# Clustered attention: staging of head pairs doubled, the first pair's load and argmax split, and a new order

## The chip, the cores and the metric

The kernel runs on one core of a Trainium2 chip, as one launch. The metric is device microseconds. Before the change three runs took 733.81, 740.06 and 740.70 us, median 740.06.

## The reference

Attention of 2 x 8 heads over 768 positions of 64 numbers, in which a query sees only the keys that were assigned to its cluster, followed by two feed-forward layers:

```python
q_assign = np.argmax(np.einsum('bhsd,hcd->bhsc', q_n, c_n), axis=-1)   # 16 clusters
k_assign = np.argmax(np.einsum('bhsd,hcd->bhsc', k_n, c_n), axis=-1)
mask = q_assign[:, :, :, None] == k_assign[:, :, None, :]
scores = np.where(mask, scale * np.matmul(q, k.transpose(0, 1, 3, 2)), -1000000000.0)
scores = scores - np.max(scores, axis=-1, keepdims=True)
attn = np.exp(scores); attn = attn / (np.sum(attn, axis=-1, keepdims=True) + 1e-09)
out = np.matmul(attn, v)
x = max(x @ w1, x @ w2, x @ w3) @ w_out      # 1536 tokens, 512 -> 768 -> 512
x = relu(x @ w_in) ** 2 @ w_out2             # 512 -> 2048 -> 512
```

## The kernel before

The 16 heads are worked on as eight pairs of 128 partitions (two heads of 64). Numbers are split into a rounded part and a remainder, and each product is made of several matmuls over the parts. All changes lie in the attention stage; the feed-forward layers behind it stay as they are.

For each pair p:

1. SP loads queries and keys (tq, tk, L284) and values (tv, L291). The first pair comes in two halves.
2. rq, rk round queries (times 0.125) and keys into rl (L343, L350), lq, lk make the remainders (L359, L365). rl has one buffer, and so have tq and tk.
3. Eight DMAs on SP (L375 to L378) copy rl into the two stacks, ste for the even head and stodd for the odd one, in which a head's rounded part and remainder lie on the two halves of the partitions.
4. TensorE multiplies rl with the centroids (sim, L404, two halves of six matmuls), ScalarE scales the result (simc, L409), TensorE transposes it (argt, L420), VectorE takes the argmax in five steps (arg0 to arg4, L427 to L448), TensorE transposes the one-hot result (mkt, L457; for the first pair also mkk, L462). ScalarE turns it into mask rows m (m4, L472), which SP copies into the stacks (md, L479 to L482). For the first even head they are written to the stack directly (L470, L471).
5. Each of the 12 score tiles of a pair (S, L497 and L499) takes two matmuls without and two with the mask rows. VectorE takes the row maximum (L506), ScalarE the exponential with its sum (L513). For a group of three tiles VectorE adds the guard 1e-9 to the sums (L517) and takes the reciprocal (L518). GpSimd normalizes (nrm, L528), TensorE transposes (T, L533, three at a time into one bank), ScalarE rounds (hi, L539), VectorE makes the remainder (lo, L544), and TensorE multiplies with the values (av, L553 and L554). ScalarE copies the result out (avt), GpSimd adds its halves (xr, L575) and writes it to xT (xh, xl, L581 and L587), the input of the next layer.

xT holds 4 head pairs x 2 parts x 1536 tokens. A pair of the first batch writes the first 768 tokens, one of the second batch the others.

What sets the order: the steps are put into a table of operations with their dependencies and buffers (room), and a planner in the program gives each engine's instructions their order when the program is built, by the keys in OFF and the durations in COST and COST2. On the chip each engine then works in that order, and SP and ScalarE issue their DMAs in it. warm(n) issues n small matmuls that nobody reads, with counts from WARM.

Of the kernel before, what the change touches and what calls it, by code (L numbers as in the profile page):

```python
# [45 lines left out]
}  # L46
COST = {
    "ldqk": ("sp", 0.95, 2.18), "ldv": ("sp", 0.48, 1.09), "stack": ("sp", 2.6, 3.28), "md": ("sp", 2.6, 0.55),
    "wld": ("sp", 0.95, 2.91), "clr": ("pool", 1.35, LAT), "scl": ("pool", 0.25, LAT),
    "sim": ("pe", 0.97, 0.2), "argt": ("pe", 0.35, 0.2), "mkt": ("pe", 0.35, 0.2), "S": ("pe", 0.65, 0.2),  # L50
    "T": ("pe", 0.33, 0.2), "av": ("pe", 0.33, 0.2), "m": ("pe", 0.65, 0.2),
    "simc": ("act", 0.46, LAT), "m4": ("act", 0.88, LAT), "ex": ("act", 0.88, LAT), "hi": ("act", 0.37, LAT),
    "avt": ("act", 0.75, LAT), "arg0": ("dve", 0.47, LAT), "arg1": ("dve", 0.47, LAT), "arg2": ("dve", 0.27, LAT),
    "arg3": ("dve", 0.47, LAT), "arg4": ("dve", 0.47, LAT), "mx": ("dve", 0.87, LAT), "rec": ("dve", 0.3, LAT),
    "xr": ("pool", 0.96, LAT), "xh": ("pool", 0.8, LAT), "xl": ("pool", 0.96, LAT),
# [29 lines left out]
def clustered_attention_moe(ctx, tc, qT, kT, vv, cen, w123, wo1, win, wo2, out):  # L85
# [154 lines left out]
    with ExitStack() as actx:  # L240
# [86 lines left out]
        for a, b in zip_longest(norm, parts):  # L327
            a()
            if b is not None:
                b()  # L330
# [631 lines left out]
```

## Time and profile before

| | |
|---|---|
| timed runs | 733.81, 740.06, 740.70 us |
| the profiled execution | 735.72 us, of it span 733.8 us |
| TensorE busy | 709.2 us (97%), mean granted clock 0.988 |
| VectorE busy | 577.5 us (79%) |
| GpSimd busy | 450.0 us (61%) |
| ScalarE busy | 328.9 us (45%) |

The page's busy time is an average over stages. Attention takes roughly the first 270 us. In it four engines work in turn on every group of tiles; behind it TensorE works alone for the most part. A matmul's span reaches from its start to its modelled end and overlaps the next one's, so TensorE can be called busy where it is not at its peak. Clock 1.00 stands for 2.4 GHz and 0.50 for 1.2 GHz.

### The profile page before, as it was taken

The numbers are of one execution on the slowest core, as the hardware profiler recorded it, in microseconds if no ns is written. First come the engines' busy times: TensorE is split into PE (matmuls) and PEld (weight loads), VectorE is DVE, ScalarE is ACT, GpSimd is POOL, SyncE is SP. The second block draws the span as 40 slices with busy tenths as digits, with TensorE's granted clock in tenths as the row PEclk, the third lists the DMA queues.
The fourth block names the chain that finished last, engine by engine and source line by source line (L and its number), as shares of the span: only waits on it lengthen the run. The fifth ranks groups of instructions, "written<-read, shape, count | busy, mean of one in ns | idle before, by whom it ended". The sixth has DMA issues, their size and how long they took to land.

```text
span 733.8 us, 10401 instructions
## 1 busy us (share of the span) xinstructions
PE 709.2 (97%) x3640; PEld 599.0 (82%) x3640; DVE 577.5 (79%) x946; ACT 328.9 (45%) x630; POOL 450.0 (61%) x385
## 2 busy tenths in 40 slices
PE   6879999899999999999999999999999999999998
PEld 5678988788898878888888888878888888888886
DVE  6788999799999999888988586795766777665434
ACT  4678898788989852222122112232222222323210
POOL 4546985988678767446654243376777666766540
PEclk9799999999999999999999999999999999999999
DMA  7756537355454002213221122202111111210004
GB/s 169 177 149 149 123 94 190 64 145 121 112 135 155 2 1 87 86 58 115 86 80 53 56 72 86 87 32 84 58 57 59 58 57 58 89 55 1 0 1 172
DMA packets 20244, 63.00 MB, mean 86 GB/s; under 512 B 3200, under 2 KB 3968, under 8 KB 19168
## 3 DMA queue, kind: packets, MB, share of 16 engines
q1 hardware_dynamic: 20192, 62.34, 29.8%
q8 instruction: 29, 0.48, 0.3%
q14 instruction: 23, 0.19, 0.1%
HBM read 38.83 MB, written 3.15 MB: 57 GB/s over the span
## 4 chain that ended last, share of the span: by engine, by line
PE 76%; DVE 11%; ACT 3%; SPq 3%; DMA 3%; POOL 2%; issue 2%; ACTq 0%; DVEq 0%; POOLq 0%
PE psd L236 27%; PE pss L876 18%; PE pss L236 14%; PE pss L533 4%; DVE nm L506 3%; PE psd L497 3%; PE pss L553 3%; PE pss L554 2%; PE psd L499 2%; DVE at L544 2%; PE pss L404 2%; DMA stodd<-rl 2%; POOL e L528 1%; ACT e L513 1%; SPq L377 1%
## 5 line engine op out<-in xcount | busy, mean ns | idle before, releaser
L211 POOL TENSOR_TENSOR wt<-wt,ww 128x512 f32<-128x512 f32 (+1 forms) x56 | 78.6, 1413 | 118.1 <-DVE wt L210 118.1
L876 PE MATMUL pss<-w,g 128*128 128x512 f32 (+1 forms) x582 | 134.8, 390 | 1.8 <-DVE acc L882 1.8
L236 PE MATMUL psd<-xT,whl 128*128 128x512 f32 x432 | 131.2, 390 | 0.1
L876 PEld LDWEIGHTS pss<-w,g 128*128 128x128 f32 x582 | 109.6, 190 | 24.9 <-DVE acc L882 2.3
L884 DVE TENSOR_TENSOR acc<-pss,acc 128x512 f32<-128x512 f32 (+1 forms) x85 | 58.2, 684 | 79.7 <-PE pss L876 79.6
L236 PE MATMUL psd<-yT,whl 128*128 128x512 f32 x384 | 118.3, 389 | 0.0
L544 DVE TENSOR_TENSOR at<-pss,at 128x384 fp32r<-128x384 f32 x192 | 100.1, 545 | 9.1 <-ACT at L539 7.9
L533 PE MATMUL pss<-ident,e 128*128 128x128 f32 x576 | 94.5, 275 | 6.5 <-DVE at L544 3.3
L539 ACT CAST at<-pss 128x384 fp32r<-128x384 f32 x192 | 88.3, 479 | 23.5 <-PE pss L533 19.7
L528 POOL TENSOR_SCALAR e<-e,nm 128x768 f32<-128x768 f32 x93 | 86.5, 947 | 15.5 <-DVE nm L518 12.3
L506 DVE TENSOR_REDUCE nm<-psd 128x1 f32<-128x768 f32 x96 | 90.5, 946 | 5.8 <-PE psd L499 5.3
L236 PEld LDWEIGHTS psd<-xT,whl 128*128 128x128 f32 x432 | 80.6, 188 | 16.8 <-POOL xT L587 0.5
L513 ACT ACTIVATE e<-psd,nm 128x768 f32<-128x768 f32 x96 | 87.3, 910 | 12.9 <-DVE nm L506 11.9
L533 PEld LDWEIGHTS pss<-ident,e 128*128 128x128 f32 x576 | 73.2, 141 | 16.9 <-DVE at L544 5.3
L236 PEld LDWEIGHTS psd<-yT,whl 128*128 128x128 f32 x384 | 72.1, 188 | 15.0
L899 ACT ACTIVATE rt<-psd 128x1024 f32<-128x1024 f32 x16 | 16.5, 1029 | 143.5 <-PE psd L236 141.1
L224 POOL TENSOR_TENSOR whl<-wt,whl 128x512 fp32r<-128x512 f32 (+1 forms) x40 | 58.5, 1463 | 36.1 <-ACT whl L223 36.1
L236 PE MATMUL pss<-xT,whl 128*128 128x512 f32 x216 | 80.5, 389 | 0.0
L904 POOL TENSOR_TENSOR g<-rt,g 128x768 fp32r<-128x768 f32 x32 | 67.4, 2128 | 16.4 <-ACT g L902 16.4
L553 PE MATMUL pss<-at,vs 128*128 128x384 f32 x192 | 75.2, 392 | 0.1
L236 PE MATMUL pss<-yT,whl 128*128 128x512 f32 x192 | 74.7, 389 | 0.0
L554 PE MATMUL pss<-at,vs 128*128 128x384 f32 x192 | 65.4, 340 | 1.4 <-DVE at L544 1.3
(121 smaller groups left out, 1198.2 us busy)
## 6 DMA issues: line engine op xcount, KB each, us to landing
wr<-w SPq DMA_DIRECT2D x16, 512.0 KB, 3.4
wr<-wo SPq DMA_DIRECT2D x16, 512.0 KB, 3.4
wr<-win SPq DMA_DIRECT2D x16, 512.0 KB, 3.7
ste<-rl SPq DMA_DIRECT2D x8, 576.0 KB, 4.9
ste<-rl SPq DMA_DIRECT2D x24, 192.0 KB, 5.3
stodd<-rl SPq DMA_DIRECT2D x8, 576.0 KB, 6.1
stodd<-rl SPq DMA_DIRECT2D x24, 192.0 KB, 5.9
tv<-vv SPq DMA_DIRECT2D x8, 384.0 KB, 4.3
```

Of the source, the lines that this page charges most:

```text
L211: lambda: pool.tensor_tensor(t, t, f(w), op=ALU.add),
L236: pe.matmul(pt[n], w[:, wi, c], x[:, k, xi, ch(n)], start=first and wi + xi == 0, stop=last and wi == 1)
L506: dve.tensor_reduce(nms[g][:, 0, i : i + 1], pss[s][:, :, :HS], axis=AX.XY, op=ALU.max, negate=True)
L513: act.activation(two(e), pss.pop(s)[:, :, :HS], AF.Exp, bias=nm[:, 0, i : i + 1], accum_out=nm[:, 1, i : i + 1])
L528: (pool if w == "P" else dve).tensor_scalar(e, e, r, 1.0, op0=ALU.mult, op1=ALU.mult)
L533: pe.transpose(pt[:, i * P : (i + 1) * P], et[3 * g + i][:, kt * P : (kt + 1) * P], ident)
L539: act.copy(a[:, 0, :], pts[g, kt][:, :HS])
L544: eng.tensor_tensor(a[:, 1, :], pts.pop((g, kt))[:, :HS], f(a[:, 0, :]), op=ALU.subtract)
L553: pe.matmul(avs[g][:, :HS], l, a[:, 0, :], start=kt == 0, stop=False)
L554: pe.matmul(avs[g][:, :HS], l, a[:, 1, :], start=False, stop=kt == NQ - 1)
L876: pe.matmul(pt[:, n], gs[fi][:, a, c], wspl[u_out(fi)][:, wi, n], start=fi == fs[0] and a + wi == 0, stop=fi == fs[-1] and a == 1)
L904: todo.append(lambda h=h, fi=fi: (pool).tensor_tensor(gt[:, 1, h], rt[:, h], f(gt[:, 0, h]), op=ALU.subtract))
```

## The change

- tq, tk, the mask rows (sm) get two buffers, at six for four. Odd pairs are staged (rl) in the part of xT for the second batch's tokens of head pairs 2 and 3, which only pairs 6 and 7 write.
- The first pair's two key loads go to ScalarE's DMA queue.
- The first even stack's own half is copied by ScalarE and GpSimd (own), its other half by two DMAs instead of four in all; later pairs' eight DMAs alternate between the even and the odd stack, the remainders first.
- The first pair's argmax, its transposes and its mask rows are made in two halves. The centroid norms (cn) become an operation of the planner. The first pair's lk is split between VectorE and GpSimd.
- The guard's addition goes from VectorE to ScalarE (ra).
- Warm-up matmuls: 12, 10, 36, 17 become 12, 10, 0, 20, 12, 8.
- The planner's durations and all its keys have new values.

```diff
-WARM = 12, 10, 36, 17, 0
+WARM = 12, 10, 0, 20, 12, 8, 0
-    "lk@0": "D", ...
+    "lk@0": "DP", ...
 OFF = {
-    "ldqk": -0.85, "ldv": 11.9, "ldqk+@0": 0.5, ...
+    "ldqk": 20.52, "ldv": -58.87, "ldqk+@0": 109.58, ...
 ...
+    guard = cp.tile([P, 1], F32, name="guard")
+    pool.memset(guard, 1e-9)
 ...
-                ins[p] = [ap.tile([P, S], F32, tag=t, bufs=1, name=f"{t}{p}") for t in ("tq", "tk")]
+                ins[p] = [ap.tile([P, S], F32, tag=t, bufs=2, name=f"{t}{p}") for t in ("tq", "tk")]
-            for t, src in zip(ins[p], (qT, kT)):
-                sp.dma_start(t[:, c], src[b, hp][:, c])
+            for t, src, q in zip(ins[p], (qT, kT), (sp, act if p == 0 else sp)):
+                q.dma_start(t[:, c], src[b, hp][:, c])
 ...
+                if p % 2:
+                    prep[p] = xT[:, 2:4].rearrange("p h i n -> p (h i) n")[:, :, S:]
+                else:
+                    prep[p] = ap1.tile([P, 4, S], F32R, tag="rl", name=f"rl{p}")
 ...
+        def p_own(p, i):
+            rl, t = prep[p], stack_of(p, 0)
+            if i == 0:
+                act.copy(t[0:64, 0:2, :], f(rl[0:64, 0, :]).unsqueeze(1).to_broadcast([64, 2, S]))
+            else:
+                pool.tensor_scalar(t[0:64, 2:4, :], f(rl[0:64, 1:3, :]), 1.0, 1.0, op0=ALU.mult, op1=ALU.mult)
+        def p_stack(p, *os):
+            rl = prep[p]
+            ts = {o: stack_of(p, o) for o in os}
+            for i in range(2 if p == 0 and os == (0,) else 4):
+                for o, t in ts.items():
+                    lo, hi = slice(64 * o, 64 * o + 64), slice(64 - 64 * o, 128 - 64 * o)
+                    to, fr = [((hi, 0), (lo, 3)), ((hi, 2), (lo, 1)), ((lo, slice(1, 4)), (lo, slice(0, 3))), ((lo, 0), (lo, 0))][i]
+                    sp.dma_start(f(t[to]), f(rl[fr]))
 ...
+        def tiles_of(hf):
+            t = range(NQ) if hf is None else range(NQ // 2 * hf, NQ // 2 * (hf + 1))
+            return t, slice(4 * t[0], 4 * t[-1] + 4)
 ...
+        def p_mq(p, hf):
+            act.activation(st[0][64:80, 1, half(hf)], pmk[p][0:16, half(hf)], AF.Identity, bias=m4b[0:16], scale=m4s[0:16])
+        def p_mk(p, hf):
+            dve.tensor_copy(st[0][64:80, 3, half(hf)], pmk["k"][0:16, half(hf)])
 ...
+        def a_guard(g):
+            nm = nms[g]
+            act.activation(nm[:, 2, :], nm[:, 1, :], AF.Identity, bias=guard)
         def a_rec(g):
             nm = nms[g]
-            dve.tensor_scalar_add(nm[:, 2, :], nm[:, 1, :], 1e-9)
             dve.reciprocal(nm[:, 3, :], nm[:, 2, :])
 ...
-            a = ap.tile([P, 2, HS], F32R, tag="at", bufs=4, name=f"at{g}_{kt}")
+            a = ap.tile([P, 2, HS], F32R, tag="at", bufs=6, name=f"at{g}_{kt}")
 ...
-        room = {"S": 2, ..., "at": 4, ..., "rl": 1, "clr": 2, "tqk": 1, ..., "sm": 1, ...}
+        room = {"S": 2, ..., "at": 6, ..., "rl": 2, "clr": 2, "tqk": 2, ..., "sm": 2, ...}
```

The start of ScalarE's instructions, before (cs are the centroid norms, table the loading of a function table, rl the first pair's staging, simt the scaled similarities):

```order
L114 ACT_TABLE_LOAD
L114 ACTIVATE table<-tiny 128x1
L314 ACTIVATE cs<-cs,tiny 128x1
L345 ACTIVATE rl_169<-tq_163 128x384 x2
L354 ACT_TABLE_LOAD
L354 ACTIVATE table<-tiny 128x1
L409 ACTIVATE simt_200<-pss_72,scl 64x384
L409 ACTIVATE simt_200<-pss_73,scl 64x384
```

and now:

```order
L118 ACT_TABLE_LOAD
L118 ACTIVATE table<-tiny 128x1
L319 ACTIVATE cs<-cs,tiny 128x1
L289 DMA tk_159<-kT 128x384 x2
L351 ACTIVATE rl_170<-tq_158 128x384 x2
L360 ACT_TABLE_LOAD
L360 ACTIVATE table<-tiny 128x1
L383 CAST ste_180<-rl_170 64x1536
```

The key loads stand behind the square root for cs, and the copy of the stack's own half ahead of the similarities.

GpSimd from the rounding of a new pair's queries on, before (rl_333 is pair 1, rl_521 pair 2, e_339 the third tile of the first group, e_343 to e_384 the second group, vs_382 the values of pair 1):

```order
L343 TENSOR_SCALAR rl_333<-tq_297 128x768
L350 TENSOR_SCALAR rl_333<-tk_298 128x768
L365 TENSOR_TENSOR rl_333<-tk_298,rl_333 128x384 x2
L528 TENSOR_SCALAR e_339<-e_339,nm_315 128x768
L383 TENSOR_SCALAR vs_382<-tv_335 128x6x2x64
L391 TENSOR_TENSOR vs_382<-tv_335,vs_382 128x3x128
L528 TENSOR_SCALAR e_343<-e_343,nm_337 128x768
L528 TENSOR_SCALAR e_369<-e_369,nm_337 128x768
L528 TENSOR_SCALAR e_384<-e_384,nm_337 128x768
L391 TENSOR_TENSOR vs_382<-tv_335,vs_382 128x3x128
L343 TENSOR_SCALAR rl_521<-tq_442 128x768
```

and now (rl_371 is pair 2, staging in xT pair 3, e_375 the third tile of the first group, e_379 to e_450 the second group):

```order
L349 TENSOR_SCALAR rl_371<-tq_249 128x768
L356 TENSOR_SCALAR rl_371<-tk_250 128x768
L371 TENSOR_TENSOR rl_371<-tk_250,rl_371 128x384
L399 TENSOR_SCALAR vs_398<-tv_334 128x6x2x64
L566 TENSOR_SCALAR e_375<-e_375,nm_323 128x768
L407 TENSOR_TENSOR vs_398<-tv_334,vs_398 128x3x128 x2
L371 TENSOR_TENSOR rl_371<-tk_250,rl_371 128x384
L566 TENSOR_SCALAR e_379<-e_379,nm_373 128x768
L566 TENSOR_SCALAR e_424<-e_424,nm_373 128x768
L566 TENSOR_SCALAR e_450<-e_450,nm_373 128x768
L349 TENSOR_SCALAR xT<-tq_388 128x768
L356 TENSOR_SCALAR xT<-tk_389 128x768
```

The same place among the normalizations now holds the staging of the pair after: pair 2 where pair 1 stood, pair 3 where pair 2 stood.

SP now, behind the eight copies of pair 1's stacks (tq_388 is pair 3, tq_458 pair 4, tv_441 the values of pair 2, m_485 the mask rows of pair 1); before, only pair 2's two loads stood between those copies and the mask rows:

```order
L289 DMA tq_388<-qT 128x768
L289 DMA tk_389<-kT 128x768
L296 DMA tv_441<-vv 128x768
L289 DMA tq_458<-qT 128x768
L289 DMA tk_459<-kT 128x768
L514 DMA ste_344<-m_485 16x768
L515 DMA ste_344<-m_485 16x768
L516 DMA stodd_133<-m_485 16x768
L517 DMA stodd_133<-m_485 16x768
```

The mask rows of pair 1 have moved behind three more loads.

## Rows read from the trace of the kernel before

**Rows 1.** Stages: us, busy of each engine (instructions), clock, DMA share, GB/s.

```profile
0.00:16.05 16.05, 10.44 (x107) 8.09 (x107) 10.40 (x43) 7.33 (x11) 7.88 (x25) 1.00 0.67 165
16.05:30.54 14.49, 11.74 (x40) 8.95 (x41) 8.19 (x10) 7.46 (x15) 5.75 (x7) 0.65 0.66 164
30.54:46.91 16.37, 11.74 (x83) 10.32 (x81) 12.73 (x25) 11.16 (x25) 7.39 (x8) 1.00 0.90 220
46.91:69.09 22.18, 21.87 (x142) 19.67 (x142) 20.69 (x39) 19.42 (x44) 13.90 (x17) 1.00 0.62 144
69.09:222.03 152.94, 148.72 (x962) 132.55 (x962) 141.13 (x256) 134.40 (x296) 124.50 (x132) 0.99 0.50 118
128.60:162.40 33.80, 31.07 (x194) 27.57 (x193) 27.73 (x52) 26.89 (x60) 29.57 (x32) 0.95 0.48 113
192.69:222.03 29.34, 29.14 (x194) 26.32 (x194) 27.45 (x52) 26.69 (x60) 24.87 (x28) 1.00 0.46 101
222.03:272.69 50.66, 48.52 (x306) 42.38 (x306) 48.35 (x88) 42.84 (x96) 37.70 (x38) 1.00 0.16 57
272.69:733.80 461.11, 456.12 (x2009) 377.00 (x2008) 335.97 (x490) 106.30 (x148) 252.89 (x163) 1.00 0.19 66
```

**Rows 2.** Chain of waits, 49.52 to 54: start us, us on the chain, what.

```profile
49.52 0.33 PE pss L533 x3
...
51.92 0.35 PE psd L497 x2
52.27 0.35 PE psd L499 x2
52.62 1.05 PE pss L404 x6
53.67 0.18 PE pss L553
```

**Rows 3.** Timeline of TensorE: start us, us, instruction, idle before and its releaser.

```profile
9.66 2.18 PE L128 MATMUL pss<-identb 128*128 128x128 bf16 x36
...
16.05 0.59 PE L497 MATMUL psd<-ste 128*128 128x384 f32 x2 [1.37 <-issue]
```

**Rows 4.** Timeline of GpSimd, the rounding of loaded keys (L350) and queries (L343).

```profile
6.61 0.51 POOL L350 TENSOR_SCALAR rl<-tk 128x384 fp32r<-128x384 f32 x1 [1.83 <-DMA tk<-kT]
...
24.18 0.83 POOL L343 TENSOR_SCALAR rl<-tq 128x768 fp32r<-128x768 f32 x1 [10.72 <-DMA stodd<-m]
...
44.10 0.83 POOL L343 TENSOR_SCALAR rl<-tq 128x768 fp32r<-128x768 f32 x1 [8.57 <-DMA ste<-m]
...
129.49 1.21 POOL L343 TENSOR_SCALAR rl<-tq 128x768 fp32r<-128x768 f32 x1 [6.75 <-PE pss L533]
```

**Rows 5.** Timeline of ScalarE, the square root for the centroid norms.

```profile
3.21 0.29 ACT L314 ACTIVATE cs<-cs,tiny 128x1 f32<-128x1 f32 x1 [0.98 <-DVE cs L313]
```

**Rows 6.** Timeline of SP's DMA issues: second key, first and last stacking copy.

```profile
2.58 0.43 SPq L284 DMA_DIRECT2D tk<-kT  x1
...
8.09 0.56 SPq L375 DMA_DIRECT2D ste<-rl  x1
...
17.30 1.34 SPq L378 DMA_DIRECT2D stodd<-rl  x1
```

**Rows 7.** Stages as in rows 1, two pieces of 2 us.

```profile
18.00:20.00 2.00, 0.94 (x3) 0.94 (x4) 0.84 (x1) 1.87 (x4) 0.00 (x0) 0.62 0.92 214
28.00:30.00 2.00, 1.86 (x9) 1.15 (x8) 1.53 (x2) 1.68 (x4) 2.00 (x3) 0.82 0.31 65
```

**Rows 8.** Instructions by line, 50 to 260 us: count, busy us, mean ns, idle.

```profile
L528 POOL TENSOR_SCALAR e<-e,nm 128x768 f32<-128x768 f32 x84 | 77.9, 945 | 14.7 <-DVE nm L518 11.9 <-PE pss L554 1.3 <-PE pss L533 0.8
...
L513 ACT ACTIVATION_READ_ACCUMULATOR e<-psd,nm 128x1 f32 x84 | 17.0, 202 | 0.0
...
L365 POOL TENSOR_TENSOR rl<-tk,rl 128x384 fp32r<-128x384 f32 x12 | 12.4, 1037 | 0.4
L517 DVE TENSOR_SCALAR nm<-nm 128x3 f32<-128x3 f32 x28 | 11.1, 395 | 3.0 <-ACT e L513 3.0
```

More of the change, by code (lines that the diff above doesn't have):

```diff
@@ L326, in clustered_attention_moe @@
                   for o, r, c in rc]
[L327 to L330, printed above, removed]
+        for o in parts:
+            o()
         st, vvs, prep = {}, {}, {}
@@ L413, in clustered_attention_moe, with once @@
         NB_ = NQ * 4
-        arg = {}
-        def p_argt(p):
-            t = simt.pop(p)
-            pt = ps_m(f"psn{p}")
-            for i in range(NQ):
+        argp, argm, arge, argn = {}, {}, {}, {}
+        def tiles_of(hf):
+            t = range(NQ) if hf is None else range(NQ // 2 * hf, NQ // 2 * (hf + 1))
+            return t, slice(4 * t[0], 4 * t[-1] + 4)
+        def once(have, p, make):
+            if p not in have:
+                have[p] = make()
+            return have[p]
@@ L445, in p_arg4, with arg_in @@
-        def p_arg4(p):
-            eq, m2 = arg.pop(p)
-            o = ap1.tile([P, NB_, NC], BF16, tag="oh", name=f"oh{p}")
-            dve.tensor_tensor(o, eq, m2.unsqueeze(2).to_broadcast([P, NB_, NC]), op=ALU.is_equal)
-            oh[p] = o
-        pmk, mrow = {}, {}
-        def p_mkt(p):
-            o = oh.pop(p).rearrange("p (t a) c -> p t (a c)", t=NQ)
-            pt = pmk[p] = ps_m(f"pmk{p}", BF16)
-            for i in range(NQ):
+                warm(WARM[2 + hf])
+        def arg_in(p, c):
+            return argp[p].rearrange("p (a c) -> p a c", c=NC)[:, c]
@@ L458, in p_mkt @@
             if p == 0:
[L460 to L472 removed]
+                warm(WARM[4 + hf])
@@ L484, in wearly_tmp @@
         def wearly_tmp(i):
-            return [ap.tile([P, S], F32, tag=t, bufs=1, name=f"w{t}{i}")[:, :512] for t in ("tq", "tk", "tv")]
+            return [ap.tile([P, S], F32, tag=t, bufs=1 + (t != "tv"), name=f"w{t}{i}")[:, :512] for t in ("tq", "tk", "tv")]
         NT = B * H * NQ
@@ L629, in clustered_attention_moe @@
             if p < 2:
[L630 to L632 removed]
+                pop_("clr", p_clear, (p,), [("rk", 0, 1)] * p, opens=[("clr", p)])
+            for os in [(0,), (1,)] if p == 0 else [(0, 1)]:
+                pop_("stack", p_stack, (p, *os), parts + [("clr", p)] * (1 in os and p < 2), opens=[("st", p, o) for o in os if p + o], uses=[("rl", p)])
@@ L684, in clustered_attention_moe @@
         if NPAIRS == B * HP:
-            last = [(n, NPAIRS - 1, hf) for n in ("sim", "vl", "lq", "lk") for hf in range(2)] + [("stack", NPAIRS - 1, o) for o in range(2)]
+            last = [(n, NPAIRS - 1, hf) for n in ("sim", "vl", "lq", "lk") for hf in range(2)] + [("stack", NPAIRS - 1, 0, 1)]
             wops = {}
@@ L725, in cost @@
             if n == "ldqk" and len(name) == 3:
-                return "sp", 0.95, 1.09
-            return COST[n]
+                return "sp", 0.5, 1.2
+            e, c, l = COST[n]
+            if p == 0 and len(name) == 3 and n in ("argt", "arg0", "arg1", "arg2", "arg3", "arg4", "mkt"):
+                c = c / 2 + 0.05
+            if n == "stack":
+                c, l = {(0, 0): (1.2, 1.9), (0, 1): (2.4, 5.2)}.get(name[1:], (4.6, 8.0))
+            if n == "own" and name[2]:
+                e = "pool"
+            return e, c, l
         opened = {r: [] for r in room}
@@ L751, in when @@
             t = start[n]
-            for tl in ops[n][4]:
+            for i, tl in enumerate(ops[n][4]):
                 o = opened[tl[0]]
-                k = len(o) - room[tl[0]]
+                k = len(o) - room[tl[0]] + sum(t[0] == tl[0] for t in ops[n][4][:i])
                 if k >= 0:
@@ L764, in clustered_attention_moe @@
             for e, names in ready.items():
-                can = [(max(free[e], w), ops[n][0], n) for n in names if (w := when(n)) is not None]
+                can = [(max(free[e], w), round(ops[n][0], 4), num[n], n) for n in names if (w := when(n)) is not None]
                 if can:
                     t0 = min(can)[0] + AHEAD
-                    c = min((k, t, n) for t, k, n in can if t <= t0)
+                    c = min((k, t, i, n) for t, k, i, n in can if t <= t0)
                     if pick is None or c[1] < pick[0]:
-                        pick = c[1], e, c[2]
+                        pick = c[1], e, c[3]
             t, e, n = pick
```

182 lines of the change are left out of this document (99 added, 83 removed), and 47 rows, old and new, of tables (COST2, ENG, OFF).

## Prediction

> **What bounds the kernel now.** I read the table of stages first, then TensorE's timeline where the stages differ, then the other engines' waits there. From 272.69 us on, TensorE is busy for 456.12 of 461.11 us [rows 1], and the change touches nothing behind that point. So only the attention stage ahead of it can gain or lose.
>
> In it "busy" says little, since spans overlap. I price TensorE's work from the chain of waits, in a stretch where it only ran [rows 2]: a group of three transposes 0.33 us, a score tile 0.35 + 0.35 = 0.70, a value product 0.18, two of them as two score matmuls of the same size 0.35, half a similarity 1.05. One group of three tiles is 2.10 + 6 x 0.33 + 6 x 0.35 = 6.18 us. A head pair is four groups, two similarity halves and two sets of small transposes (about 0.4 each, an estimate): 24.7 + 2.1 + 0.8 = 27.6 us. What a stage takes beyond its work, I call lost. Counted by the program's order, the stages of [rows 1] lose:
> - 0 to 16.05 (up to the first score tile): 8.0 work, 8.0 lost.
> - 16.05 to 30.54 (first transposes): seven tiles and one similarity, 7.0 work, 7.5 lost, at a granted clock of 0.65.
> - 30.54 to 46.91: 10.7 work, 5.6 lost.
> - 46.91 to 69.09: 20.3 work, 1.9 lost.
> - 69.09 to 222.03, five pair periods: 5 x 27.6 = 138.1 work, 14.8 lost. The worst period, 128.60 to 162.40, loses 6.2; the best, 192.69 to 222.03, 1.7.
> - 222.03 to 272.69: 44.9 work, 5.7 lost.
>
> In sum 43.5 us. The change can only take from these, and 13 warm-up matmuls (75 to 62) at 2.18 / 36 = 0.06 us [rows 3], 0.8 us.
>
> The reasons stand in GpSimd's timeline. Its rounding of a pair's queries (L343) waits 10.72, 8.57 and 6.75 us [rows 4], for a load that stood behind the stacking copies on SP's queue, or for the single rl to be read out. The last names TensorE as releaser, which a wait for several semaphores may do wrongly. GpSimd runs in order: the normalizations queued behind such a wait come late, then the transposes.
>
> **Part by part.**
>
> *First keys on ScalarE's queue.* In ScalarE's new order both key loads stand behind the square root of the centroid norms, which ends at 3.21 + 0.29 = 3.50 us [rows 5]. SP issued the second key at 2.58 and GpSimd used it at 6.61, 4.0 later [rows 4, 6]. Issued at 3.93 it comes no earlier than 7.9. Now the second pair's queries and keys and the first values, 1.18 MB, are issued on SP meanwhile; at the 220 GB/s of a stage with full DMA [rows 1] that is 5.4 us, all or none of it ahead. So the key is 1.3 to 6.7 us later. I take 2, near the low end, since the transfers issued ahead of the keys have moved for over a microsecond by then. What the first tile saves: today TensorE waits 1.37 us there with "issue" as releaser [rows 3], when the masks are written and only the last copy of the even stack is out. The change copies the own half of that stack on ScalarE and GpSimd, so that wait goes, but the own copy on GpSimd now stands ahead (64x1536, about two of the 0.83 us ops of [rows 4], 1.7 us; it is done while VectorE works on the argmax). The argmax in halves has five more instructions but starts after half the similarities: -1 to +0.5, I take 0. **First tile at 16.05 + 2 - 1.4 = 16.7** (15 to 21).
>
> *Up to the first transposes.* Now the order is six tiles, the second pair's similarity and its small transposes, half of the third pair's similarity: 7.7 us of work. The third normalization of group 0 stands on GpSimd behind the staging of pair 2 (0.83 + 0.83 + 1.04 + 0.83 = 3.5 us [rows 4, 8]; the last is the values' rounding, priced as the queries'). Pair 2's load stands on SP behind six stack copies, not eight; eight took from 8.09 to 18.64 [rows 6], 10.6 us, by bytes two thirds of it 7.0 from about 9, so it is issued at 16 where its counterpart was issued at 18.7, and GpSimd may go on at 24.18 - 2.7 = 21.5. With 3.5, 0.4 for the key and 0.9 for the normalization the transposes start at 26.4, if the clock holds. If it is at 0.5 from the first tiles on, as today (0.62 in 18 to 20, still 0.82 in 28 to 30 [rows 7]), 7.7 us of work takes 15.5 and they start at 32. I take **28**: lost 28 - 7.2 - 7.7 = 13.1 instead of 15.5, **-2.4** (-4 to +1.7).
>
> *Pair 2 staged ahead.* The 8.57 us wait is gone there: pair 2's two copies are made before the first transposes. Next late is pair 3's load, behind one whole stack of 10.6 us, and pair 1's mask, behind that stack and five loads of 393 KB: 1.97 MB at 220 GB/s, 8.9 us, issued from about 19, so it is due at 38.5 to 40; TensorE wants it at 28 + 12.5 = 40.5. I put 2.5 lost for 5.6: **-3.1** (0 to -4.5).
>
> *Double rl, double tq and tk.* In later pairs the loads stand one pair earlier on SP, and odd pairs go to the part of xT that only pairs 6 and 7 write as results. Waits like the 6.75 have a whole period of slack. *Guard add.* On VectorE it costs 395 ns [rows 8], 1.6 us a period on an engine that is busy for 27.5 of 29.34; on ScalarE I price it as the accumulator read, 202 ns, 0.8 us a period, to 26.7 [rows 1]. So afterwards TensorE has 27.6, ScalarE 27.5, VectorE 25.9 a period. What a period loses is bounded by 0 and the best one's 1.7; I take 1.5, near that row, since ScalarE has become as full as TensorE: five periods lose 7.5 for 14.8, **-7.3** (-12 to +1). at and sm with more buffers cost nothing and are in this.
>
> *The end.* The last two periods have the same work and the weights' bits on VectorE in other places: **-0.4** (+-2).
>
> Sum: -0.8 - 2.4 - 3.1 - 7.3 - 0.4 = -14.0. The profiled execution took 735.72 (span 733.8, 1.9 around it): 721.7. Two of the three timed runs lie 4 to 5 us above it, the third 1.9 below, median 740.06. I can't place that difference in the trace and add half of it: **724 us**.
>
> **The rivals.**
> - *Keys late, clock low.* The first tile at 20 and half the clock to 32 and beyond: startup +2 instead of -2.4, then 728.4. For: nothing in the order lets the keys start before 3.50. Against: GpSimd and VectorE, not TensorE, set that stage today. The Trainium skill (DMA: Bandwidth & Descriptors, section "Issuing engines are not separate DMA queues") says that DMAs started by several engines run on the same 16 engines and interleave, and that a second queue saves only issue time. By that rule the keys share with the 1.18 MB and this rival is the likelier; no row here shows two queues. 0.15.
> - *ScalarE becomes the bound.* The periods lose what they lose now (14.8): 724 + 7.3 = 731. For: 27.5 of about 29 us busy, and the guard now sits between an exponential and the reciprocal, with every cast behind it. Against: VectorE was fuller and is freed of twice that. 0.15.
> - *The double staging isn't one.* If a copy into xT had to wait for stacking copies that read its other part, the 6.75 us waits would return: about 729. In the new order only GpSimd's and no DMA's completion stands before it. 0.04.
> - *Slower: the mask behind SP's queue.* SP serves in order, and pair 1's mask now stands behind loads that wait for GpSimd's copies of pair 2. If a mask comes over 2.6 us after TensorE could start its pair, in each of seven periods, 18 us are lost again and the kernel is at 742 or over; a slip of 4 us each gives 752. For: pair 1 has only the slack worked out above. Against: later masks stand behind the stack alone, a period ahead of use. 0.08.
>
> **How the numbers follow.** The forecast, 714 to 729, has 0.58. The first three rivals add up to 733, with the 4 us by which runs differ to 736; left out are what is below 714 and the slower rival, together some 0.17. So the range is **714 to 736**. One per cent, 7.4 us, is about what a measurement of this kernel can tell from no change. Below 732.7 lies the forecast (0.56 of it) and most of the first three rivals: 0.77. Within 1%: 0.17; above 747.5: 0.06.
>
> **What would show it.** First transposes near 28 us and granted clock at 1.0 before 26; no L343-like wait over 2 us on GpSimd after 50 us; pair periods of 29 us; VectorE some 1.5 us less busy a period and ScalarE 0.8 more; the last value product near 259. Wrong would be: first tile after 19, a score tile of a new pair waiting for a DMA, or periods that still take 30 with ScalarE releasing most waits.

## The result, and the profile after

The changed kernel took 729.9 us (median of 11 runs, 727.51 to 732.59), the kernel before 739.83 (median of 11, 733.81 to 741.85): ratio 0.9888, 95% interval 0.9859 to 0.9917. Forecast were 724 us and a range of 714 to 736. The profiled execution took 729.35 us, of it span 727.3, against 733.8 before. Every ratio below is to the kernel before on the same chip.

From here on pairs are counted from 1. The text ahead of the result counts them from 0, as the code's p does, so that its "pair 2" is the third. The stages of the changed kernel, cut at the same events as [rows 1] to within 0.35 us: first score tile, first transposes, last transposes ahead of pair 2's first tile, pair 2's first value product, pair 7's (five pair periods, with a slow and a fast one of them below), the rest of attention, the layers behind. Columns: us, busy time (instructions) of TensorE, its weight loads, VectorE, ScalarE and GpSimd, granted clock, DMA share, GB/s.

```profile
0.00:23.75 23.75, 13.41 (x94) 9.71 (x94) 13.73 (x49) 8.04 (x13) 15.18 (x33) 0.90 0.66 184
23.75:33.97 10.22, 9.29 (x52) 7.92 (x49) 7.69 (x13) 7.34 (x14) 4.96 (x6) 0.90 0.73 166
33.97:49.31 15.34, 13.93 (x92) 11.97 (x91) 13.79 (x24) 13.86 (x33) 11.06 (x13) 1.00 0.87 232
49.31:70.24 20.93, 20.93 (x141) 19.29 (x140) 20.92 (x37) 20.18 (x48) 15.61 (x17) 1.00 0.50 113
70.24:216.57 146.33, 143.17 (x954) 129.56 (x953) 135.94 (x232) 136.33 (x314) 115.61 (x124) 1.00 0.49 118
130.02:160.54 30.52, 29.19 (x196) 26.22 (x194) 27.68 (x47) 27.85 (x64) 24.69 (x27) 1.00 0.43 97
189.48:216.57 27.09, 27.02 (x186) 24.89 (x185) 25.10 (x44) 26.04 (x62) 19.05 (x22) 1.00 0.46 108
216.57:266.87 50.30, 46.88 (x298) 41.71 (x297) 45.80 (x79) 42.98 (x101) 37.16 (x38) 1.00 0.15 55
266.87:727.30 460.43, 454.79 (x2011) 376.28 (x2009) 337.89 (x490) 106.37 (x148) 251.23 (x162) 1.00 0.19 66
```

The first tile comes 7.70 us later than before (23.75 for 16.05). All the gain lies behind it: five periods take 146.33 us for 152.94, and VectorE's share of them fell from 141.13 to 135.94 while ScalarE's rose from 134.40 to 136.33.

The start, in windows of 2 us (columns as above):

```profile
4.00:6.00 2.00, 1.51 (x10) 0.85 (x8) 0.79 (x4) 1.35 (x3) 0.00 (x0) 1.00 0.90 301
6.00:8.00 2.00, 0.00 (x0) 0.00 (x0) 0.00 (x0) 1.99 (x3) 0.00 (x0) 1.00 0.82 276
8.00:10.00 2.00, 0.00 (x0) 0.00 (x0) 0.00 (x0) 0.45 (x1) 0.30 (x1) 1.00 0.51 192
10.00:12.00 2.00, 0.68 (x2) 0.51 (x3) 1.76 (x4) 0.00 (x0) 1.25 (x3) 1.00 0.02 7
18.00:20.00 2.00, 0.22 (x3) 0.23 (x3) 1.98 (x5) 0.00 (x0) 1.87 (x4) 0.72 0.95 195
20.00:22.00 2.00, 2.00 (x18) 1.49 (x16) 1.92 (x3) 0.66 (x1) 1.81 (x5) 0.50 0.92 266
26.00:28.00 2.00, 2.00 (x13) 1.57 (x12) 1.29 (x2) 1.60 (x3) 0.58 (x1) 1.00 0.66 97
```

From 6 to 9.7 us TensorE, VectorE and GpSimd do nothing, while the DMA engines move 276 GB/s; then the traffic is over (7 GB/s) and work begins. From 18.9 us TensorE's granted clock is at 0.50, its lower level, where the mask transposes and the first tile stand, after a stretch from 17.7 in which TensorE waited 2.03 us for VectorE; it is 1.00 again from 25.7. The trace's clock record begins at 15.48 us, and ahead of that the column's 1.00 is no measurement (the last section): the eleven similarity matmuls at 11.32 took 3.78 us, where before they took 2.45 at a recorded 1.00. Whether the gap had a part in the later fall is not shown.

Timelines of the same stretch: start us, us, engine, instruction, idle before and its releaser. ScalarE and its queue, and SP's first stacking copies:

```profile
3.63 0.29 ACT L319 ACTIVATE cs<-cs,tiny 128x1 f32<-128x1 f32 x1 [1.41 <-DVE cs L318]
3.63 0.95 ACTq L289 DMA_DIRECT2D tk<-kT  x2
...
12.07 1.18 SPq L394 DMA_DIRECT2D ste<-rl  x2
```

GpSimd, the rounding of the first keys and, later, of queries (pairs 6, 7 and 8):

```profile
9.70 0.51 POOL L356 TENSOR_SCALAR rl<-tk 128x384 fp32r<-128x384 f32 x1 [6.43 <-DMA tk<-kT]
10.87 0.77 POOL L356 TENSOR_SCALAR rl<-tk 128x384 fp32r<-128x384 f32 x1 [0.66 <-DMA tk<-kT]
...
90.06 0.83 POOL L349 TENSOR_SCALAR xT<-tq 128x768 fp32r<-128x768 f32 x1 [4.81 <-DMA stodd<-xT]
...
119.82 0.83 POOL L349 TENSOR_SCALAR rl<-tq 128x768 fp32r<-128x768 f32 x1 [4.79 <-DMA stodd<-rl]
...
150.28 0.83 POOL L349 TENSOR_SCALAR xT<-tq 128x768 fp32r<-128x768 f32 x1 [5.42 <-DMA stodd<-xT]
```

TensorE, similarities, first mask transposes, first tile and first transposes:

```profile
11.32 3.78 PE L420 MATMUL pss<-rl,cb 128*64 128x384 f32 x11 [5.54 <-DVE rl L365]
...
19.78 0.50 PE L490 MATMUL pss<-identb,oh 128*32 128x128 bf16 x3 [2.03 <-DVE oh L478]
...
23.75 0.99 PE L532 MATMUL psd<-ste 128*128 128x384 f32 x2
...
33.97 1.47 PE L571 MATMUL pss<-ident,e 128*128 128x128 f32 x9
```

[Rows 4] had the second half of the first keys used at 6.61; here it is 10.87, TensorE is idle for 5.54 us until 11.32, and SP's first stacking copy is issued at 12.07 for 8.09 [rows 6]. The waits of 10.72, 8.57 and 6.75 us in [rows 4] are gone, but three of about 5 us stand at other pairs.

Instructions by line, 50 to 260 us, for those of [rows 8] (count, busy us, mean ns, idle); L552 is the guard on ScalarE:

```profile
L566 POOL TENSOR_SCALAR e<-e,nm 128x768 f32<-128x768 f32 x86 | 78.9, 932 | 23.8 <-DVE nm L556 17.1 <-PE psd L534 6.6
...
L548 ACT ACTIVATION_READ_ACCUMULATOR e<-psd,nm 128x1 f32 x85 | 17.1, 201 | 0.0
...
L552 ACT ACTIVATE nm<-nm,guard 128x3 f32<-128x3 f32 x29 | 8.9, 307 | 0.0
```

The guard costs 307 ns on ScalarE, not the 202 of the accumulator's read by which I had priced it. A normalization costs what it did (932 ns for 945), and waits mostly for VectorE's reciprocals (L556).

### The profile page after: what moved, and what is told of

It is laid out like the page before. It is cut to its first block, busy times and chain, and to the rows that moved or that the text cites. A ratio compares the mean times of both kernels' runs of the same rounds, so it can differ in the third digit from the quotient of the medians.

```text
span 727.3 us, 10349 instructions
## 1 busy us (share of the span) xinstructions
PE 702.4 (97%) x3627; PEld 596.4 (82%) x3627; DVE 575.8 (79%) x919; ACT 335.1 (46%) x664; POOL 450.8 (62%) x388
## 4 chain that ended last, share of the span: by engine, by line
PE 77%; DVE 11%; POOL 5%; DMA 3%; issue 2%; ACT 1%; SPq 0%; DVEq 0%; POOLq 0%; ACTq 0%
PE psd L240 28%; PE pss L936 18%; PE pss L240 14%; PE pss L571 5%; DVE at L582 3%; PE pss L591 3%; DVE nm L541 3%; PE pss L592 3%; PE psd L532 3%; PE psd L534 3%; POOL e L566 2%; PE pss L420 1%; DMA tk<-kT 1%; DMA stodd<-rl 1%; DVE rt L961 1%
## 5 line engine op out<-in xcount | busy, mean ns | idle before, releaser
L936 PE MATMUL pss<-w,g 128*128 128x512 f32 (+1 forms) x582 | 133.2, 387 | 1.8 <-DVE acc L942 1.8
L582 DVE TENSOR_TENSOR at<-pss,at 128x384 fp32r<-128x384 f32 x192 | 99.2, 544 | 11.7 <-ACT at L577 10.5
L577 ACT CAST at<-pss 128x384 fp32r<-128x384 f32 x192 | 87.1, 478 | 15.3 <-PE pss L571 10.6
L959 ACT ACTIVATE rt<-psd 128x1024 f32<-128x1024 f32 x16 | 16.5, 1029 | 141.8 <-PE psd L240 139.5
L591 PE MATMUL pss<-at,vs 128*128 128x384 f32 x192 | 78.2, 407 | 0.0
L592 PE MATMUL pss<-at,vs 128*128 128x384 f32 x192 | 64.8, 338 | 0.1
```

Of the source, the lines that this page charges most:

```text
L577: act.copy(a[:, 0, :], pts[g, kt][:, :HS])
L582: eng.tensor_tensor(a[:, 1, :], pts.pop((g, kt))[:, :HS], f(a[:, 0, :]), op=ALU.subtract)
L591: pe.matmul(avs[g][:, :HS], l, a[:, 0, :], start=kt == 0, stop=False)
L592: pe.matmul(avs[g][:, :HS], l, a[:, 1, :], start=False, stop=kt == NQ - 1)
L936: pe.matmul(pt[:, n], gs[fi][:, a, c], wspl[u_out(fi)][:, wi, n], start=fi == fs[0] and a + wi == 0, stop=fi == fs[-1] and a == 1)
```

## The experiments

For all of them, read from the traces: start of the first score tile, of the first transposes, and the eight pairs' length from that first tile to the first product of the next layer, which follows the last score tiles.

| kernel | first tile | transposes | eight pairs | ratio to before | interval |
|---|---|---|---|---|---|
| before | 16.05 | 30.54 | 243.84 | 1 | |
| changed | 23.75 | 33.97 | 227.99 | 0.9888 | 0.9859 to 0.9917 |
| keys on SP | 16.56 | 26.46 | 227.83 | 0.9829 | 0.9784 to 0.9873 |
| keys first on ScalarE | 18.07 | 27.89 | 228.33 | 0.9816 | 0.9781 to 0.9850 |
| argmax whole | 23.70 | 36.62 | 230.85 | 0.9943 | 0.9912 to 0.9973 |
| start order | 21.81 | 34.61 | 230.36 | 0.9872 | 0.9828 to 0.9917 |
| guard on VectorE | 23.25 | 32.59 | 229.55 | 0.9927 | 0.9906 to 0.9948 |
| keys on SP, start order | 16.51 | 25.84 | 226.94 | 0.9873 | 0.9814 to 0.9932 |
| keys on SP, later staging | 16.16 | 26.84 | 224.13 | 0.9786 | 0.9739 to 0.9833 |
| both and start order | 18.43 | 29.59 | 223.79 | 0.9760 | 0.9720 to 0.9801 |
| and halves apart | 20.35 | 33.05 | 225.41 | 0.9818 | 0.9780 to 0.9856 |
| before, double staging | 16.44 | 29.46 | 244.66 | 1.0054 | 1.0023 to 1.0084 |
| before, six at | 16.56 | 30.95 | 244.08 | 0.9989 | 0.9955 to 1.0023 |
| changed, four at | 23.85 | 33.40 | 238.52 | 1.0049 | 1.0023 to 1.0075 |

Against the kernel before, "eight pairs" overstates what the pairs won: the new order also puts the next layer's first product closer behind the last score tile (2.3 us behind the start of that tile's last matmuls, for 5.1). From the first tile to the last value product it is 258.56 us before and 244.68 in the changed kernel, 13.9 us less. The starts hang on TensorE's clock as well, which differs from one profiled execution to the next, so that one or two microseconds between two first tiles need not come from the edit.

### Where the keys are issued

```diff
-            for t, src, q in zip(ins[p], (qT, kT), (sp, act if p == 0 else sp)):
+            for t, src, q in zip(ins[p], (qT, kT), (sp, sp)):
```

> The changed kernel, with the first pair's key loads back on SP's queue (order there: queries, keys, queries, keys, then the second pair's loads); nothing else moves. Theory 1 (keys late): in the changed kernel the keys are issued at 3.63 us on ScalarE and share the DMA engines with pair 2's queries and keys and the values, so the second key is used at 10.87 us where before it was used at 6.61. From SP it should be used at 6.3 to 7.3, VectorE's and TensorE's start follow one for one: first score tile at 19.5 to 20.5 for 23.75, first transposes at 30 to 31.5 for 33.97, about 726 us by timed runs (-4 on the changed kernel's 729.9). Theory 2 (VectorE's own chain between the keys and the masks sets the first tile: halved argmax of 5.0 us for 2.8, remainders ahead of the norms): the keys come early but the first tile stays at 22 or later; about 729. Theory 3: loads of pair 2 simply move behind and what is won is lost again at the first transposes (33 to 34): 730.

723.65 us. GpSimd's two roundings of the first keys, the first mask transposes and the first tile:

```profile
4.34 0.51 POOL L356 TENSOR_SCALAR rl<-tk 128x384 fp32r<-128x384 f32 x1 [1.07 <-DMA tk<-kT]
6.83 0.55 POOL L356 TENSOR_SCALAR rl<-tk 128x384 fp32r<-128x384 f32 x1 [1.98 <-DMA tk<-kT]
...
13.92 0.50 PE L490 MATMUL pss<-identb,oh 128*32 128x128 bf16 x3 [0.17 <-DVE oh L478]
...
16.56 0.60 PE L532 MATMUL psd<-ste 128*128 128x384 f32 x2
```

Theory 1, and by more than it asked for: 7.19 us at the first tile, 7.3 of the span. Behind the first tile nothing changed (227.83 for 227.99), so a late start is paid in full. That is read from one profiled execution of each; by the timed runs it is 4.4 to 6.3 us (by the ratios 0.9829 and 0.9888, whose intervals overlap a little, and by the medians). From the first key to the first tile it is 12.22 us here and 14.05 in the changed kernel. Of these 1.8 us, 0.5 lie ahead of the first mask transposes (9.58 us after the first key for 10.08), where VectorE's argmax was slower, and 1.3 behind them (2.64 for 3.97), where TensorE's clock was at 0.50 in the changed kernel and at 1.00 here.

The other way to earlier keys, on ScalarE's queue:

```diff
-    act.activation(table, tiny, AF.Sqrt)
...
+            if p == 0 and hf == 1:
+                act.activation(table, tiny, AF.Sqrt)
+                act.activation(cs[:, 1:2], cs[:, 0:1], AF.Sqrt, bias=tiny)
...
-        act.activation(cs[:, 1:2], cs[:, 0:1], AF.Sqrt, bias=tiny)
```

> The changed kernel with its first key loads still on ScalarE's queue, but issued as ScalarE's first instructions, ahead of the loading of the function table and of the square root for the centroid norms, which follow them. If the keys are late because of their place behind the square root (issue at 3.63), they are now issued near 1 us and used by 6.5 to 7.5; first score tile 19.5 to 21, time like that of the version with the keys on SP, 726. If they are late because a second queue shares the DMA engines with SP's 1.18 MB of other loads, whatever the issue time, the second key is still used after 9, the first tile stays above 22, and 729 to 730. The square root comes some 1.5 us later, about 5, which the norm chain on VectorE at 11.97 can take.

723.66 us. ScalarE's queue and GpSimd's first keys:

```profile
0.72 0.89 ACTq L288 DMA_DIRECT2D tk<-kT  x2
...
3.48 0.51 POOL L357 TENSOR_SCALAR rl<-tk 128x384 fp32r<-128x384 f32 x1 [0.22 <-DMA tk<-kT]
4.60 0.51 POOL L357 TENSOR_SCALAR rl<-tk 128x384 fp32r<-128x384 f32 x1 [0.61 <-DMA tk<-kT]
```

Issued 2.9 us earlier, the second key comes 6.3 us earlier: the place behind the square root, not the second queue, made it late. The two queues together gave little speed: the last of the first pair's four loads was used at 6.35 (the queries' second half), with everything on SP at 6.83 (the second key). The first tile is 1.5 us later than with SP in spite of the earlier keys. Up to the first mask transposes nothing was won (14.10 us for 13.92): ScalarE came to the first scaling of the similarities at 9.81 (9.20), behind its table loads and its copy of the stack. From there to the first tile it is 3.97 us for 2.64, with the clock falling (0.58 in this row) to its lower level:

```profile
12.00:14.00 2.00, 1.47 (x18) 1.20 (x15) 2.00 (x8) 0.00 (x0) 1.94 (x3) 0.58 1.04 215
```

It fell at 12.3 us, after TensorE was busy for only 1.15, 0.99 and 1.01 of each 2 us from 6 to 12, and came back at 19.1; with the keys on SP it is recorded as 1.00 from 14.7 on.

### The halves and VectorE's order

The first pair's argmax in whole (here and below, ahead_of(n, m) takes a step out of the planned order and puts it ahead of another):

```diff
+        ahead_of(("mkt", 0, 1), ("mq", 0, 0))
...
+            if n[0] in ("arg0", "arg1", "arg2", "arg3", "arg4") and n[1:] == (0, 0):
+                continue
+            if n[0] in ("arg0", "arg1", "arg2", "arg3", "arg4") and n[1:] == (0, 1):
+                ops[n][1](0)
...
```

> The changed kernel with the first pair's argmax in whole, as before the change (five VectorE instructions instead of ten), its one-hot transposes and mask rows behind it; all else in its place. The halves take 15.65 to 20.62 = 5.0 us on VectorE, before the whole took 9.77 to 12.61 = 2.8. If the halving costs (fixed cost of each instruction over what the earlier start wins), the argmax now ends 1 to 2 us earlier, the first tile comes at 22 to 22.8, and the time is 728 to 729. If the earlier start of the first half pays for its extra instructions, as I forecast (0 within -1 to +0.5), the first tile comes at 23.5 to 24.7, 730.

733.61 us, slower than the changed kernel. VectorE after the argmax, and TensorE's first tile:

```profile
22.82 0.55 DVE L503 CAST ste<-pss 16x384 fp32r<-16x384 bf16 x1 [2.95 <-PE pss L490]
23.40 2.21 DVE L365 SCALAR_TENSOR_TENSOR xT<-tq,xT 128x384 fp32r<-128x384 f32 x2
25.62 0.55 DVE L503 CAST ste<-pss 16x384 fp32r<-16x384 bf16 x1
```

```profile
26.22 0.44 PE L534 MATMUL psd<-ste 80*128 80x384 f32 x1 [1.75 <-DVE ste L503]
```

The first tile began at 23.70, as the second expectation had it (23.5 to 24.7), but its time of 730 was missed, since the tile stopped half way for the masks' second half. That copy is 25.62 for 23.67 in the changed kernel, because the first half's came at 22.82 for 20.65 and the next pair's remainder stands between them. The argmax itself ended earlier in whole (19.87 for 20.62 us); the first copy waited for the second transposes, which stand behind twelve warm-up matmuls. The first transposes came 2.65 later, but not all of that is the edit's: the next pair's similarities started 1.3 later (27.45 for 26.13) and took 1.3 longer, at a granted clock of 0.58 for 1.00. So by the traces the halves win some 1.3 us in this order, by the mask copies and not by the argmax, where the forecast was 0; the timed runs (0.9943 for 0.9888) name about 4, and what else is in that is open.

```diff
+        ahead_of(("cn", 0), ("lq", 0, 0))
+        ahead_of(("lk", 0, 0), ("lk", 0, 1))
+        ahead_of(("mk", 0, 1), ("lq", 1, 1))
```

> The changed kernel with three steps in another place in VectorE's order at the start, nothing else changed: the centroid norms and the queries' remainder stand ahead of the first keys' remainder (which waits 5.36 us for the keys, to 10.24), and the second half of the mask rows stands ahead of the remainder of the second pair's queries (2.41 us). Theory 1 (VectorE's order makes the late keys cost double: work that doesn't need the keys stands behind the wait for them): first similarity's scaling ready about 2 us earlier, and the mask rows 2.4 us earlier than now: first tile at 19.5 to 20.5, time 726. Theory 2 (the transfer of the keys alone sets it): the first tile gains only the 2.4 of the mask rows, 21.3, or nothing, 23.75, since then the own copies, the stack's DMAs or the clock end last: 729.

727.27 us; its ratio can't be told from the changed kernel's. The first tile came 1.94 earlier, near the 21.3 of theory 2, and the first transposes 0.64 later: the second pair's remainder now holds up its similarity (0.78 us of TensorE's wait at 24.41), and the clock was at 0.50 from 30.6 to 34.1 us. This is the slowest of its four runs.

> The changed kernel with the first keys on SP's queue and, as well, VectorE's three steps of the run before in their other place (centroid norms and the queries' remainder ahead of the first keys' remainder, second mask half ahead of the second pair's remainder). With the keys on SP alone the first tile came at 16.56, its mask half on VectorE ended at 17.46 and the score matmul waited 0.19 us for it. Theory 1 (with early keys VectorE's order bounds the start): first tile at 15.2 to 15.8 and all behind it earlier by the same, 722.5 to 723. Theory 2 (the steps moved are off the path, since TensorE's warm-up matmuls and ScalarE's two mask copies end at 16.6 to 16.9 anyway): first tile 16.4 to 16.7, 723.5 or, as in the run with the order alone, first transposes later than 26.46 because the remainders of pair 2 now come late: 724 to 726.

This is that edit together with the keys on SP: 727.03 us, runs from 720.84 to 728.52. In the profiled one, the fastest, the first tile did not move (16.51 for 16.56), the transposes came 0.62 earlier. Theory 2 for the first tile; whether the order gains anything stays open, since runs of one kernel differ by more.

### What the pairs gained

```diff
-            act.activation(nm[:, 2, :], nm[:, 1, :], AF.Identity, bias=guard)
+            dve.tensor_scalar_add(nm[:, 2, :], nm[:, 1, :], 1e-9)
```

> The changed kernel with the guard's addition back on VectorE, each instruction in the place where ScalarE's stood; nothing else moves. VectorE gets 395 ns and ScalarE loses 307 ns, four times a pair. Theory 1 (VectorE's load bounds the pair periods, so taking 1.6 us off it is a part of what the periods won): the seven periods between the first score tiles of pairs 1 and 8 get longer by 0.5 to 1.5 us each, 733 to 739 for 729.9. Theory 2 (ScalarE is as full, and the periods are set by the order and TensorE): periods as they are within 0.3 us, 729 to 731, or shorter by up to 1 us each with ScalarE freed, 724.

730.8 us. Eight pairs take 1.56 us more (1.0 to the last value product): 0.2 a pair, not 0.5 to 1.5, so Theory 2. It does not stand in every pair: pairs 3 to 6 differ by at most 0.06 us, pair 2 takes 29.77 for 28.69. The guard's move is at most a tenth of what the pairs won.

The part alone that I had named as their cause, on the kernel before:

```diff
-                ins[p] = [ap.tile([P, S], F32, tag=t, bufs=1, ...) for t in ("tq", "tk")]
+                ins[p] = [ap.tile([P, S], F32, tag=t, bufs=2, ...) for t in ("tq", "tk")]
...
+                if p % 2:
+                    prep[p] = xT[:, 2:4].rearrange("p h i n -> p (h i) n")[:, :, S:]
...
```

> The kernel before the change with one part of the change alone: tq and tk with two buffers, and odd pairs staged in the unused part of xT. Every engine's order stays the kernel before's. Theory 1 (the single staging place costs the kernel before its long periods): GpSimd's waits of 10.72, 8.57 and 6.75 us at the rounding of queries fall, the period from the fourth pair's (33.8 us from first score tile to first score tile) comes to 30 to 31, and the second and third pair's start gain 2 to 5: 728 to 732 by fast comparison with 736 to 740. Theory 2 (the order, written for one staging place, asks for the loads and copies as late as before, so the waits only change their name): within 2 us of the kernel before. Theory 3: the copies into the second place start earlier and their loads and stack DMAs come ahead of mask rows on SP: slower, by up to 5 us.

738.73 us: not faster, but half a per cent slower. GpSimd's waits there, 45 to 260 us (line, releaser: us in total, times, longest):

```profile
POOL xT L346 <- DMA tq<-qT: 12.2, 3, 6.1
...
POOL rl L346 <- DMA stodd<-m: 10.9, 1, 10.9
```

The rounding waits for its own load now, which the old order issues late. The wait changed its name, as theory 2 says; by the medians the loss, 3.9 us, is more than its 2 and lies within the 5 of theory 3, whose cause (loads ahead of the mask rows) is not shown.

```diff
-            a = ap.tile([P, 2, HS], F32R, tag="at", bufs=6, name=f"at{g}_{kt}")
+            a = ap.tile([P, 2, HS], F32R, tag="at", bufs=4, name=f"at{g}_{kt}")
```

> The changed kernel with four buffers again for the transposed parts (at), in the changed kernel's order. Of the 15.9 us that eight pair periods won (243.84 to 227.99 from first score tile to the last pair's last), the guard's move accounts for 1.6 and the double staging alone, in the order of before, for nothing; what is left lies in the new order and in buffers that it was made for. Theory 1 (the order runs the transposes further ahead of the value products and needs the six buffers): periods longer by 0.5 to 1.5 us each, 734 to 742 for 729.9. Theory 2 (four were enough, as I forecast: more buffers cost and bring nothing): 729 to 731.

740.24 us, all of the gain gone: Theory 1. ScalarE's rounding (L577) from 49 to 260 us, in the changed kernel:

```profile
ACT at L577 <- PE pss L571: 7.3, 21, 2.5
```

and with four buffers, with TensorE's wait that follows from it:

```profile
ACT at L577 <- PE pss L592: 16.7, 35, 1.1
...
PE psd L532 <- ACT e L548: 8.0, 13, 1.5
```

L592 is the value product that frees a buffer. ScalarE stands 35 times for it, the exponentials queue behind, and the score tiles behind those. Eight pairs: 10.5 us more.

> The kernel before the change with one part of it alone: six buffers instead of four for the transposed parts (at), every engine's order as before. In the changed kernel's order four buffers cost 10.3 us (740.24 for 729.9): ScalarE's rounding then waited 35 times for a value product, 16.7 us in all, and TensorE for exponentials behind it. Theory 1 (the buffers carry the gain of the periods whatever the order): eight periods fall from 243.84 to 230 to 236 us, 726 to 732. Theory 2 (the order of before was planned for four and reads out a buffer before it asks for the next, so that two more stand unused; order and buffers gain only together): periods 241 to 244, within 2 us of the kernel before.

The same edit backwards on the kernel before (four to six): 734.67 us for 736.0, no difference. Neither the buffers nor the staging place gains by itself. Counted to the last value product, the new order with four buffers gains 2.0 us of the pairs' 13.9 (256.53 us from the first tile) and loses them at the start; the order with six has all of it. The new order with a single staging place was not tried, since in it pair 4's queries would be rounded ahead of the normalizations that free that place; what double staging carries there is not shown.

### Where the three staging waits went

```diff
+        for p, m in ((5, ("rk", 5)), (6, ("lk", 6, 0)), (7, ("lk", 7, 0))):
+            ahead_of(("rq", p), m)
+            if p > 5:
+                ahead_of(("rk", p), m)
```

> The changed kernel with the first keys on SP's queue, and with GpSimd's rounding of queries and keys for pairs 6 to 8 moved behind the next three normalizations, which now stand behind it. As it is, that rounding waits 5.44, 4.82 and 5.09 us for the last copies that read the same staging place (two pairs before), and TensorE waits 0.9, 0.7 and 0.8 us for a normalization shortly after each. Theory 1 (these waits hold up the normalizations): GpSimd's waits there fall below 2 us, TensorE's three waits go, last value product some 2 us before 261.08, 721.5 to 722.5 for 723.65. Theory 2 (the waits fall into slack, since the normalizations behind them have their sums late as well): within 0.5 us of the version with the keys alone.

718.95 us: Theory 1, and more than it asked for. Waits from 45 to 260 us in the version with the keys on SP alone:

```profile
POOL xT L349 <- DMA stodd<-xT: 10.5, 2, 5.4
...
POOL rl L349 <- DMA stodd<-rl: 4.8, 1, 4.8
...
PE pss L571 <- POOL e L566: 3.0, 4, 0.9
```

and with the later staging:

```profile
POOL rl L349 <- PE pss L592: 0.7, 1, 0.7
...
PE pss L571 <- DVE at L582: 3.2, 4, 2.0
```

The staging waits are gone, and so is TensorE's wait for a normalization. Pairs 4 to 6 (first tile to first tile) take 28.56, 28.56 and 28.54 us for 30.42, 30.11 and 28.85 and pair 3 28.79 for 29.8; eight pairs gain 3.7 us, more than the 3.0 that TensorE's timeline named (by the ratios, 0.9786 for 0.9829, it is 3.2, with intervals that overlap).

> The changed kernel with the first keys on SP's queue, GpSimd's rounding for pairs 6 to 8 behind the next normalizations (together 718.95) and VectorE's three steps at the start in their other place. With the keys alone this order brought the first transposes from 26.46 to 25.84 and the last value product from 261.08 to 260.15, while its first tile stayed. Theory 1 (these 0.6 to 0.9 us add to the later staging's): last value product at 256.0 to 256.4 for 256.97, 718.0 to 718.4. Theory 2 (they are lost in the second pair, whose remainder comes late): within 0.4 us, 718.6 to 719.3.

718.64 us (716.01 to 721.59), the fastest of all, and not to be told from the run before it. The profiled execution has its start at clock 0.50 from 10 to 18 us and its first tile 2.3 us later than the run before, whose clock stayed at 1.00, and eight pairs 0.3 us shorter; the timed runs don't separate the theories.

```diff
+        order.remove(("own", 0, 0))
+        order.insert(order.index(("simc", 0, 1)) + 1, ("own", 0, 0))
+        ahead_of(("argt", 0, 0), ("sim", 0, 1))
+        ahead_of(("simc", 0, 0), ("argt", 0, 0))
```

> The run before this one, with the first half's transposes for the argmax ahead of the second half of the similarities on TensorE, and ScalarE's own copy of the stack behind both scalings. I had forecast that the halved argmax starts after half of the similarities; in the changed kernel's order both halves stand ahead of the first transposes, so that it starts only after both (transposes at 9.70 in the version with keys and later staging, similarities 6.08 to 9.77). Theory 1 (that order keeps the halves from gaining): VectorE's first reduction at 8.2 to 8.8 for 10.14, the second half's one-hot done 0.4 to 1 us before 14.44, first tile at 15.2 to 15.7 for 16.16, 0.4 to 0.9 us less in all. Theory 2 (the second half sets the first tile and starts no earlier, since TensorE now waits for the first scaling, 0.6 us): first tile at 16 to 16.5, no gain.

722.69 us: worse. TensorE's transposes for the second half:

```profile
12.94 0.58 PE L446 MATMUL pss<-ident,simt 64*128 64x64 f32 x3 [0.67 <-ACT simt L425]
```

They came 1.8 us later than in the run before (11.12), behind two waits of 0.67 for a scaling and similarities that started late; the first tile moved to 20.35 for 18.43. In both the twenty warm-up matmuls took 2.32 us, the time at the lower clock. No gain, as theory 2 says, but its first tile (16 to 16.5) was missed too: it did not name this loss.

## Why the prediction was right, and where it was not

- **The sign, range and time**: right, 729.9 in 714 to 736; 5.9 us above the forecast. By the profiled run it is 7.65 (729.35 for 721.7): some 6.0 from the start, 2.2 from the five periods, 1.1 from the end, 1.0 back from the two stages between start and periods, and 0.7 back from the layers behind. One of its own signs of being wrong came, a first tile after 19.
- **First tile at 16.7** (range 15 to 21): 23.75. The step that failed is "I take 2, near the low end" for the keys. By the landings in the profile the second pair's queries and keys were in at 6.7 and 9.2 us, the first key at 9.6, the values at 10.4 and the second key at 10.8: all of the 1.18 MB landed ahead of the second key, which was used at 10.87, 4.3 late. The first key, not priced by itself, came 5.4 late (9.70 for 4.27), and the chain behind it was 1.8 longer than with the keys on SP: 0.5 where VectorE's argmax met GpSimd's staging of pair 2 (the last section), 1.3 behind it at the lower clock. The 1.4 us of the stack's last copy did not show: from the first key it is 11.78 before and 12.22 with the keys on SP. That comparison is not clean either, since the eleven similarity matmuls took 2.45 us before and 3.78 there.
- **The rival with late keys and a low clock** (728.4) gave the time better than the forecast, in part by luck: the first tile came later than its 20, and the clock, low "to 32 and beyond" in it, was back at 25.7. The Trainium skill (DMA: Bandwidth & Descriptors, "Issuing engines are not separate DMA queues") says beside it that a second queue saves only the time of issuing. The keys agree: on the same queue the second came at 4.60 or 10.87, by the issue time.
- **First transposes at 28, -2.4**: 33.97, +3.4, all from the first tile; from tile to transposes it is 10.22, and 9.90 with the keys on SP.
- **Pair 2 staged ahead, -3.1** (counted from 0): right in size. That stage lost 2.9 us for the 2.5 forecast; the mask of pair 1 held nothing up. No run takes this part away by itself. The slower rival did not happen.
- **Double rl, tq and tk, -7.3**: the five periods lost 9.7 us instead of 7.5 (146.33 less 136.7 of work, as 8 half similarities stand in them now and not 10), so the size was near, but the reason was wrong in part. The step that failed is "at and sm with more buffers cost nothing and are in this": in the new order six buffers for at carry 10.5 us of the eight pairs. Double staging alone, in the old order, carries none; what it carries in the new one is not shown. "Waits like the 6.75 have a whole period of slack" failed too: the new order stages pairs 6 to 8 so early that each waits 4.8 to 5.4 us for the copies of two pairs before.
- **Guard**: 307 ns for 202; the move is worth at most 1.6 us in eight pairs. ScalarE did not become the bound.
- **The end, -0.4**: it lost 6.4 for 5.7, +0.7.

## What to carry to other kernels

Before a load is moved to another engine's queue, look at what that engine does ahead of it: the place in its order sets the issue time, and here most of what was issued earlier elsewhere was moved first. Extra buffers showed nothing until the order asked for them, and the new order lost its gain without them, so try them together and take each away afterwards. A transfer or a rounding that is placed earlier than its buffer comes free is a wait for everything queued behind it on that engine; three of them cost 3.7 us here.

## What the runs showed of the hardware

Some of VectorE's instructions took longer beside GpSimd's. In the changed kernel's start:

```profile
18.58 1.15 DVE L478 TENSOR_TENSOR oh<-eq,m 128x192 bf16<-128x192 bf16 x1
...
21.23 2.41 DVE L365 SCALAR_TENSOR_TENSOR xT<-tq,xT 128x384 fp32r<-128x384 f32 x2
```

The first took 0.34 us in the version with the keys on SP, the second is 1.2 us each for 0.55 in the same line at 31.85, with GpSimd idle; GpSimd was subtracting (L371, 18.39 to 19.50 and 20.96 to 21.96; L407 from 21.92) or rounding then. The Trainium skill (SBUF — State Buffer, "SBUF: two separate sides") says that GpSimd shares a port pair with VectorE's instructions of two inputs in SBUF, and that the one that starts first holds it to its end. Both of these have two such inputs, and the first row agrees: it ended 0.23 us after the subtraction that had started before it.

Twenty warm-up matmuls took 2.31 us with the keys on SP and 1.29 with the later staging, both in windows whose clock column says 1.00, and 2.32 with both and the start order, where it says 0.50:

```profile
11.43 2.31 PE L132 MATMUL pss<-identb 128*128 128x128 bf16 x20
...
10.94 1.29 PE L132 MATMUL pss<-identb 128*128 128x128 bf16 x20
...
11.60 2.32 PE L132 MATMUL pss<-identb 128*128 128x128 bf16 x20
```

The traces' clock records begin at 14.72, 9.54 and 5.20 us: ahead of its first entry the column says 1.00 with nothing recorded. So the matmuls' own time is the better sign at a kernel's start, and by it the first of these rows ran at the lower level.
